# A build-time list scheduler with other durations and due times, the low part of v on GpSimd, row instructions on VectorE alone

## The chip, the core and the metric

The kernel runs on one core of one Trainium2 chip. A core has five engines that work side by side, each through its own queue, in the order in which the program lists its instructions: TensorE (PE; its weight loads are PEld), VectorE (DVE), ScalarE (ACT), GpSimd (POOL) and SyncE (SP), which here only issues DMAs. TensorE writes to PSUM. An engine whose next instruction waits for a semaphore stands still, also when a later instruction of its queue could run. The metric is the device time of one execution in microseconds (us).

## The reference

Three networks follow one another. The first is attention in which a query sees only keys of its own hash bucket (signs of six projections), for 2 batches x 8 heads, 768 positions, head size 64:

```python
q_bits = (np.einsum('bhsd,dk->bhsk', q, proj) > 0).astype(np.int64)
k_bits = (np.einsum('bhsd,dk->bhsk', k, proj) > 0).astype(np.int64)
mask = q_bucket[:, :, :, None] == k_bucket[:, :, None, :]
scores = scale * np.matmul(q, k.transpose(0, 1, 3, 2))
scores = np.where(mask, scores, -1000000000.0)
scores = scores - np.max(scores, axis=-1, keepdims=True)
attn = np.exp(scores)
attn = attn / (np.sum(attn, axis=-1, keepdims=True) + 1e-09)
return np.matmul(attn, v).astype(np.float32)
```

Its output, 2 x 768 x 512, goes through a channel mix (x is blended with the position before, then `k = relu(xk @ w_k)`, `v = k*k @ w_v`, `r = sigmoid(xr @ w_r)`, result `r * v`, inner size 1024), and that through a token mix of rank 32 and a two-matrix MLP (512 to 2048 to 512) with residuals.

## The kernel before

Every operand of a matmul is split into a high and a low part, so that a product is made of three (high x high, high x low, low x high). The weights arrive as 64-bit floats and are put together from their two words by "conversion jobs" (`conv_load`, `conv_scale`, `conv_bits`, `conv_sum`, `conv_h`, `conv_l`), each over SP, ACT, DVE, POOL, ACT and DVE or POOL.

The work has two stages. The first is attention, with the first four conversion jobs and the shift of the first channel mix woven in. It has 16 heads, and each head six tiles of 128 queries, 96 tiles in all. For a head, k and q are loaded (`load_head`), split (`prep_H` makes the high part `hl`, `prep_L` the low one), transposed on TensorE (`prep_T`), copied from PSUM to `yk`, `yq` (`prep_E`), moved by DMA to `xk`, `xq` (`prep_x`), projected (`prep_z`), cut to bits `zt` (`prep_bits`), and the bits are moved by four small DMAs into `xk`, `xq` (`prep_mask`); v is scaled by a power of two (`v_max` to `v_scale`) and split into `V2` (`prep_v`). For a tile n: scores on TensorE into one of three PSUM buffers `ps` (`scores`, L467 and L468), the row maximum (`row_max`, L472, DVE), two instructions on one column (`row_scale`, L476, and `row_bias`, L480), the exponential (`exps`, L486, ACT), and then the split and transposition of the probabilities. Two tiles of six go by TensorE (`flip`, `flip_part1`, `flip_part2`, through a `ps` buffer), four by `part1` (ACT or POOL), `part2` (POOL) and a transposing DMA (`transp`, L501). Last, the probabilities times v (`weighted`, L537, 18 matmuls). After the last head, matmuls of the channel mix begin (`r`), and everything from there on is written out by hand: matmuls on TensorE without a break, with the remaining conversion jobs on the other engines.

The order of the first stage is set by `Plan.order`, a list scheduler that runs while the kernel is built. Each operation is added with its engines and a duration on each, the operations it comes after, a due number (the tile number plus an entry of the table `DUE`), and the buffers that it takes and gives back (`SLOTS`). At each step of a simulated clock the scheduler takes, of the operations that are ready, the one with the lowest due number whose engine and buffers are free; of two engines it takes the one with the shorter duration. The order found is the order of the queues on the chip. DMAs are operations of "sp": the queue is free again 0.1 us after an issue, and the wires are one resource.

## Time and profile before

| What | Value |
|---|---|
| Median of 3 runs | 771.44 us (771.07 to 777.1) |
| The profiled execution: its own time | 771.87 us |
| its span, first to last instruction | 770.1 us |
| mean granted TensorE clock | 0.959 of full speed |
| first and last scores of the first stage | 29.1 and 298.8 us |

The profiled execution's time is 1.8 us above its span and 0.4 us above the median, so sums made on it carry over to the median nearly unchanged. In the rows below an instruction is given as line, engine, operation, and "out<-in" with the names of the tiles.

### The profile page before, as it was taken

To read this page: it belongs to the slowest core of one execution; us is meant where nothing else is said; L and a number is where in the kernel's file an instruction comes from. 1 tells how busy PE (TensorE), PEld (TensorE's weight loads), DVE (VectorE), ACT (ScalarE), POOL (GpSimd) and SP (SyncE) were. 2 spreads that over 40 slices of the span, in tenths; PEclk is the share of its full clock that TensorE was granted. 3 is DMA by queue.
4 is the path that set the end of the run, shared out by engine and by line. 5 is a ranking of instruction groups with operands and counts; after the bars stand their busy time and mean duration, and the time that the engine had idled before them with its cause. 6 is when DMAs were issued, how large, how long until landed. Compare 5 with 4: busy or idle time off the path is not lost.

```text
span 770.1 us, 12423 instructions
## 1 busy us (share of the span) xinstructions
PE 692.0 (90%) x4748; PEld 583.9 (76%) x4748; DVE 479.1 (62%) x778; ACT 372.8 (48%) x607; POOL 367.0 (48%) x365
## 2 busy tenths in 40 slices
PE   3688887887787886999999999999999999999997
PEld 2577777776676775888878888877888888888886
DVE  4776787778989778789977997864643111131112
ACT  3566676665566656586646866643531111111010
POOL 2786797776899778557734754542320000000000
PEclk9598999999989996999999999999999999999999
DMA  8367888886576689233201333232301000010001
GB/s 245 97 134 142 178 190 147 169 154 124 114 144 124 113 185 207 83 123 95 66 28 55 110 113 106 82 110 78 114 28 55 0 1 1 0 55 1 0 1 54
DMA packets 130732, 73.69 MB, mean 96 GB/s; under 512 B 104625, under 2 KB 123953, under 8 KB 130673
## 3 DMA queue, kind: packets, MB, share of 16 engines
q1 hardware_dynamic: 130528, 72.71, 40.0%
q8 instruction: 37, 0.61, 0.3%
q10 hardware_dynamic: 144, 0.20, 0.1%
q14 instruction: 23, 0.18, 0.1%
HBM read 37.10 MB, written 3.15 MB: 52 GB/s over the span
## 4 chain that ended last, share of the span: by engine, by line
PE 60%; DVE 11%; POOL 9%; DMA 9%; issue 5%; ACT 3%; SPq 2%; POOLq 0%; DVEq 0%; ACTq 0%
PE ps L745 9%; PE ps L747 9%; PE ps L746 9%; PE pt L745 7%; PE pt L747 7%; PE pt L746 7%; DMA pT<-p 5%; PE pt L537 3%; POOL p L168 3%; DVE nm L472 2%; DVE w L168 2%; PE ps L467 2%; ACT p L486 2%; PE ps L468 1%; POOL p L352 1%
## 5 line engine op out<-in xcount | busy, mean ns | idle before, releaser
L820 DVE SCALAR_TENSOR_TENSOR hl<-pt,hl 128x512 fp32r<-128x512 f32 x48 | 33.2, 691 | 170.8 <-ACT hl L819 170.8
L819 ACT ACTIVATE hl<-pt 128x512 fp32r<-128x512 f32 x48 | 28.7, 598 | 185.6 <-PE pt L747 185.6
L168 POOL TENSOR_TENSOR cx<-cx,raw 128x512 int32<-128x512 int32 (+2 forms) x55 | 81.6, 1484 | 76.1 <-DVE cx L220 69.5
L747 PE MATMUL ps<-w,hl 128*128 128x512 f32 x288 | 113.6, 395 | 2.7 <-DVE hl L734 2.5
L745 PE MATMUL ps<-w,hl 128*128 128x512 f32 x288 | 114.9, 399 | 1.2 <-ACT y L715 1.1
L746 PE MATMUL ps<-w,hl 128*128 128x512 f32 x288 | 113.1, 393 | 0.0
L168 POOL TENSOR_TENSOR p<-p,p 128x768 f16<-128x768 f32 x64 | 108.4, 1696 | 4.8 <-ACT p L350 2.9
L486 ACT ACTIVATE p<-ps,nm 128x768 f32<-128x768 f32 x96 | 93.6, 989 | 34.1 <-DVE nm L480 14.9
L472 DVE TENSOR_REDUCE nm<-ps 128x1 f32<-128x768 f32 x96 | 90.1, 950 | 29.6 <-PE ps L468 28.3
L467 PE MATMUL ps<-xk,xq 76*128 76x384 f32 x192 | 78.1, 407 | 19.1 <-ACT p L486 12.0
L537 PE MATMUL pt<-v,pT 128*128 128x65 f16 (+1 forms) x1728 | 72.8, 199 | 21.7 <-DMA pT<-p 16.6
L537 PEld LDWEIGHTS <-pT 128*128 128x128 f16 x1728 | 65.5, 102 | 33.6 <-DMA pT<-p 21.8
L745 PE MATMUL pt<-ut,w 128*128 128x512 f32 x192 | 75.5, 393 | 0.0
L747 PE MATMUL pt<-ut,w 128*128 128x512 f32 x192 | 75.0, 391 | 0.0
L746 PE MATMUL pt<-ut,w 128*128 128x512 f32 x192 | 74.9, 390 | 0.0
L468 PE MATMUL ps<-yk,yq 128*128 128x384 f32 x192 | 70.6, 368 | 0.0
L747 PEld LDWEIGHTS ps<-w,hl 128*128 128x128 f32 x288 | 54.0, 188 | 18.3 <-DVE hl L734 6.5
L168 DVE TENSOR_TENSOR w<-cx,w 128x512 fp32r<-128x512 f32 (+2 forms) x53 | 61.8, 1166 | 8.0 <-ACT w L260 5.3
L745 PEld LDWEIGHTS ps<-w,hl 128*128 128x128 f32 x288 | 54.1, 188 | 15.4 <-issue 1.7
L746 PEld LDWEIGHTS ps<-w,hl 128*128 128x128 f32 x288 | 54.1, 188 | 10.2
L467 PEld LDWEIGHTS ps<-xk,xq 76*128 76x128 f32 x192 | 40.7, 212 | 23.4 <-ACT p L486 16.0
L216 DVE SCALAR_TENSOR_TENSOR raw<-raw 128x512 uint32<-128x512 uint32 (+2 forms) x55 | 52.8, 961 | 2.9 <-ACT raw L212 2.9
(166 smaller groups left out, 1417.0 us busy)
## 6 DMA issues: line engine op xcount, KB each, us to landing
raw<-in_moe_w_ch_dram SPq DMA_DIRECT2D x32, 512.0 KB
raw<-in_moe_w_k_dram SPq DMA_DIRECT2D x8, 512.0 KB
raw<-in_moe_w_v_dram SPq DMA_DIRECT2D x8, 512.0 KB
nk<-in_k_dram SPq DMA_DIRECT2D x16, 192.0 KB
nv<-in_v_dram SPq DMA_DIRECT2D x16, 192.0 KB
xk<-yk SPq DMA_DIRECT2D x16, 192.0 KB
xq<-yq SPq DMA_DIRECT2D x16, 192.0 KB
nq<-in_q_dram SPq DMA_DIRECT2D x15, 192.0 KB
```

The costliest lines, as they stand in the source:

```text
L168: eng.tensor_tensor(out=out, in0=a, in1=b, op=op)
L216: nc.vector.scalar_tensor_tensor(out=raw[:, :, 0], in0=raw[:, :, 1], scalar=0x80000000, in1=raw[:, :, 0], op0=ALU.bitwise_and, op1=ALU.bit ...
L467: nc.tensor.matmul(s_ps[:, j, 0:G], d["xq"][:, qc], d["xk"][:, c], start=True, stop=False)
L468: nc.tensor.matmul(s_ps[:, j, 0:G], d["yq"][:, qc], d["yk"][:, c], start=False, stop=True)
L472: nc.vector.tensor_reduce(out=nm[:, 0:1], in_=tl[n]["s"][:, :, 0:G], axis=AX.XY, op=ALU.max, negate=True)
L486: nc.scalar.activation(p, tl[n].pop("s")[:, :, 0:G], AF.Exp, bias=nm[:, 2:3], scale=nm[:, 1:2])
L537: nc.tensor.matmul(o[:, 0:d], pT[:, part, kt, :], V[:, kt, a, 0:d], start=(kt == 0 and (part, a) == (0, 0)), stop=(kt == NT - 1 and part = ...
L745: nc.tensor.matmul(o, sh, mh, start=first, stop=False)
L746: nc.tensor.matmul(o, sh, ml, start=False, stop=False)
L747: nc.tensor.matmul(o, sl, mh, start=False, stop=last)
L819: nc.scalar.activation(hl[:, 0], self.o, AF.Relu)
L820: nc.vector.scalar_tensor_tensor(out=hl[:, 1], in0=self.o, scalar=0.0, in1=f(hl)[:, 0], op0=ALU.max, op1=ALU.subtract)
```

## The change

No arithmetic changes in kind, and the second stage is not touched. Three functions change. `prep_v` made the high part of v on ACT or POOL straight from the loaded v and its scale, and the remainder on DVE with one two-operation instruction that scaled v again; now ACT scales v in place, ACT copies the result to the high part, and POOL subtracts. `row_scale` and `row_bias`, which could go to DVE or POOL, go to DVE alone. In the scheduler, almost all durations and half of `DUE` have other values, an issue on "sp" keeps that queue for 0.5 or 1.4 us, several operations lose one of their engines (the high parts of k and q and the copies to `xT` are ACT's alone after the first head; the shift's first step too), and loads get predecessors: k, q and v of a head, and the early weight loads, wait in the plan for moves of earlier heads.

```diff
-DUE = {"ld": -11, "h": -9, "lo": -6, "tr": -11, "es": -8, "xs": -7, "z": -5, "bits": -8.5, "mask": -5,
+DUE = {"ld": -15, "h": -8.5, "lo": -7, "tr": -11, "es": -8, "xs": -5, "z": -5, "bits": -10.5, "mask": -8,
...
                 if e == "sp":
-                    clock[e] = now + 0.1
-                    wire = max(wire, now + 1.3) + cost
-                    op.end = wire + 0.8
+                    clock[e] = now + (1.4 if cost > 2.2 else 0.5)
+                    wire = max(wire, now + 1.2) + cost
+                    op.end = wire + 0.6
...
-    def prep_v(i, part, e):
-        v, sc, h = hd[i]["nv"], v_scale_of(i), V2[i % 2][:, :, 0, 0:D]
-        if part:
-            nc.vector.scalar_tensor_tensor(
-                out=V2[i % 2][:, :, 1, 0:D], in0=v, scalar=sc, in1=h, op0=ALU.mult, op1=ALU.subtract
-            )
-            hd[i].pop("nv")
-        elif e == "act":
-            nc.scalar.activation(h, v, AF.Identity, scale=sc)
+    def prep_v(i, part):
+        v, h = hd[i]["nv"], V2[i % 2][:, :, 0, 0:D]
+        if part == 0:
+            nc.scalar.activation(v, v, AF.Identity, scale=v_scale_of(i))
+        elif part == 1:
+            nc.scalar.activation(h, v, AF.Copy)
         else:
-            nc.gpsimd.tensor_scalar(h, v, sc, None, ALU.mult)
+            minus("pool", V2[i % 2][:, :, 1, 0:D], hd[i].pop("nv"), h)
...
-        due = i * NT
+        due = i * NT if i else -50
         y_done, xs, masks, toks = [], [], [], {}
+        gate = ready_of[max(i - 2, 0)][1] if i else []
...
-            ld = add({"sp": 0.8}, lambda e, i=i, s=s: i and load_head(i, s), due=due + DUE["ld"] if i else -99, take=[n_s])
-            h = add({"act": 0.52, "dve": 0.4}, lambda e, i=i, s=s: prep_H(i, s, e), [ld], due + DUE["h"], take=[hl_s])
+            ld = add({"sp": 0.8}, lambda e, i=i, s=s: i and load_head(i, s), gate, due + DUE["ld"] if i else -99, take=[n_s])
+            h = add({"act": 0.53, "dve": 0.4} if i == 0 else {"act": 0.53}, lambda e, i=i, s=s: prep_H(i, s, e), [ld], due + DUE["h"], take=[hl_s])
...
-                v1 = add({"act": 0.52, "pool": 0.55}, lambda e, i=ii: prep_v(i, 0, e), [v_sc, v_ld[ii]], d + DUE["v1"], take=[v_s2])
-                v2_of[ii] = add({"dve": 0.6}, lambda e, i=ii: prep_v(i, 1, e), [v1], d + DUE["v2"], free=[nv_s2])
+                v0 = add({"act": 0.52}, lambda e, i=ii: prep_v(i, 0), [v_sc, v_ld[ii]], d + DUE["v1"] - 0.5)
+                v1 = add({"act": 0.52}, lambda e, i=ii: prep_v(i, 1), [v0], d + DUE["v1"], take=[v_s2])
+                v2_of[ii] = add({"pool": 1.0}, lambda e, i=ii: prep_v(i, 2), [v1], d + DUE["v2"], free=[nv_s2])
...
-            sl = add({"dve": 0.165, "pool": 0.25}, lambda e, n=n: row_scale(n, e), [mx], n + DUE["sl"])
-            bi = add({"dve": 0.225, "pool": 0.3}, lambda e, n=n: row_bias(n, e), [sl], n + DUE["bi"])
+            sl = add({"dve": 0.17}, lambda e, n=n: row_scale(n), [mx], n + DUE["sl"])
+            bi = add({"dve": 0.23}, lambda e, n=n: row_bias(n), [sl], n + DUE["bi"])
...
-        last = ld = add({"sp": 2.1}, lambda e, j=j: conv_load(j), [last_s[-10] if j >= KD else None], due - 10, take=[raw_s])
+        last = ld = add({"sp": 2.1}, lambda e, j=j: conv_load(j), [last_s[-10] if j >= KD else ready_of[j][0][0]], due - 10, take=[raw_s])
```

Counted over the queues: DVE loses 19 high parts of k and q, 9 copies to `xT`, all 16 remainders of v and 12 shift multiplications, and gains 86 row instructions; POOL loses those 86 and 8 scalings of v and gains the 16 subtractions; ACT gains the 19, the 9, the shift's and, for v, has 32 instructions where it had 8. In TensorE's queue the scores that stand ahead of a tile's `weighted` are, over tiles 6 to 89, 5.65 more than its own number before and 6.60 now.

On SyncE, at the start of the program, before (tiles carry their buffer numbers; `raw` is a weight, `nk`, `nq` and `nv` are loads of heads; the last two rows are the mask moves of head 0):

```order
L199 DMA raw_168<-in_moe_w_r_dram 128x1024
L292 DMA nk_179<-in_k_dram 128x384
L292 DMA nq_193<-in_q_dram 128x384
L387 DMA xk_202<-yk_185 64x768
L387 DMA xq_205<-yq_200 64x768
L292 DMA nk_234<-in_k_dram 128x384
L292 DMA nq_242<-in_q_dram 128x384
L199 DMA raw_257<-in_moe_w_r_dram 128x1024
L387 DMA xk_268<-yk_238 64x768
L387 DMA xq_277<-yq_249 64x768
L407 DMA xk_202<-zt_220 12x384 x2
L407 DMA xq_205<-zt_220 12x384 x2
```

The same place now (its rows three to six are the moves of head 0):

```order
L574 DMA mu_k_142<-in_moe_mu_k_dram 128x4x1
L574 DMA mu_r_145<-in_moe_mu_r_dram 128x4x1
L387 DMA xk_175<-yk_163 64x768
L387 DMA xq_178<-yq_173 64x768
L407 DMA xk_175<-zt_189 12x384 x2
L407 DMA xq_178<-zt_189 12x384 x2
L292 DMA nv_195<-in_v_dram 128x384
L292 DMA nv_197<-in_v_dram 128x384
L292 DMA nk_199<-in_k_dram 128x384
L292 DMA nq_201<-in_q_dram 128x384
L199 DMA raw_208<-in_moe_w_r_dram 128x1024
L292 DMA nv_215<-in_v_dram 128x384
```

The moves of head 0 now stand ahead of every load but those of head 0 and of three small tensors; before, 16 loads of heads and weights stood ahead of the mask moves, six of them in this block.

On DVE, some 33 tiles into the first stage, before (`nm` holds a tile's maximum, scale and bias):

```order
L472 TENSOR_REDUCE nm_1781<-ps_1764 128x1
L476 TENSOR_SCALAR nm_1781<-nm_1781 128x1
L472 TENSOR_REDUCE nm_1808<-ps_1783 128x1
L544 TENSOR_SCALAR rl_1821<-pt_1564,vsc_1460 128x6
L449 SCALAR_TENSOR_TENSOR v2_0_132<-nv_325,vsc_1460,v2_0_132 128x6x64
L548 RECIPROCAL rl_1821<-rl_1821 128x6
L556 TENSOR_TENSOR xn_1831<-pt_1564,rl_1821 128x6x64
L168 TENSOR_TENSOR pT_1833<-ps_1810,pT_1833 128x768
L472 TENSOR_REDUCE nm_1867<-ps_1835 128x1
L472 TENSOR_REDUCE nm_1880<-ps_1869 128x1
L417 TENSOR_REDUCE vmax_388<-nv_1829 128x1
L352 CAST hl_k_1938<-nk_1392 128x6x64
```

The same place now (L469, L473 and L477 are maximum, scale and bias):

```order
L469 TENSOR_REDUCE nm_1660<-ps_1640 128x1
L473 TENSOR_SCALAR nm_1660<-nm_1660 128x1
L469 TENSOR_REDUCE nm_1689<-ps_1662 128x1
L477 TENSOR_SCALAR nm_1660<-nm_1660 128x1
L473 TENSOR_SCALAR nm_1689<-nm_1689 128x1
L477 TENSOR_SCALAR nm_1689<-nm_1689 128x1
L469 TENSOR_REDUCE nm_1748<-ps_1720 128x1
L473 TENSOR_SCALAR nm_1748<-nm_1748 128x1
L477 TENSOR_SCALAR nm_1748<-nm_1748 128x1
L400 TENSOR_SCALAR zt_1777<-pt_1753,thr_118 108x384
L469 TENSOR_REDUCE nm_1788<-ps_1770 128x1
L473 TENSOR_SCALAR nm_1788<-nm_1788 128x1
```

Now each maximum is followed by both row instructions within a few places; before, four maxima have one row instruction here, the others were POOL's or stand behind a later maximum.

On ACT, around the exponentials of tiles 24 to 27, before:

```order
L486 ACTIVATE p_1400<-ps_1360,nm_1371 128x768
L350 ACTIVATE p12_1448<-p_1400 128x768
L486 ACTIVATE p_1458<-ps_1374,nm_1394 128x768
L454 ACTIVATE v2_0_132<-nv_154,vsc_1460 128x6x64
L486 ACTIVATE p_1477<-ps_1384,nm_1446 128x768
L486 ACTIVATE p_1511<-ps_1453,nm_1474 128x768
L350 ACTIVATE p12_1536<-p_1511 128x768
L520 ACTIVATE pT_1545<-ps_1529 128x768
```

The same place now (L449 scales a loaded v in place, L451 makes its high part):

```order
L483 ACTIVATE p_1398<-ps_1276,nm_1321 128x768
L350 ACTIVATE hl_q_1425<-nq_1248 128x6x64
L449 ACTIVATE nv_230<-nv_230,vsc_1432 128x384
L449 ACTIVATE nv_397<-nv_397,vsc_1432 128x384
L451 ACTIVATE v2_0_132<-nv_230 128x6x64
L449 ACTIVATE nv_734<-nv_734,vsc_1432 128x384
L449 ACTIVATE nv_1033<-nv_1033,vsc_1432 128x384
L483 ACTIVATE p_1472<-ps_1393,nm_1434 128x768
L483 ACTIVATE p_1520<-ps_1427,nm_1450 128x768
L451 ACTIVATE v2_1_134<-nv_397 128x6x64
```

Four instructions for v, and one for q, now stand in a row between two exponentials, and a fifth behind the pair that follows.

## Rows read from the trace of the kernel before

**Rows 1.** The page: the chain that ended last, by engine.
```profile
PE 60%; DVE 11%; POOL 9%; DMA 9%; issue 5%; ACT 3%; SPq 2%; POOLq 0%; DVEq 0%; ACTq 0%
```

**Rows 2.** Stretches: length, busy time by engine (instructions), clock, DMA share.
```profile
0.00:29.00 29.00, 12.81 (x45) 9.42 (x46) 16.61 (x53) 12.44 (x24) 12.36 (x18) 0.81 0.73 208
29.00:304.00 275.00, 221.23 (x2546) 196.97 (x2545) 217.53 (x399) 178.01 (x255) 215.53 (x239) 0.91 0.74 148
304.00:330.00 26.00, 24.91 (x192) 20.74 (x192) 18.39 (x26) 15.83 (x30) 16.07 (x14) 0.99 0.39 106
330.00:770.00 440.00, 433.02 (x1968) 356.73 (x1968) 226.59 (x302) 166.53 (x301) 123.08 (x96) 1.00 0.17 55
```

**Rows 3.** The chain, 29 to 304 us, by line.
```profile
by line: DMA pT<-p 14.3%; issue 7.9%; POOL p L168 7.5%; PE pt L537 7.5%; DVE nm L472 6.8%; PE ps L467 5.0%; ACT p L486 4.4%; PE ps L468 4.0%; POOL p L352 3.8%; SPq L407 3.7%; PE pt L376 2.8%; DMA nv<-in_v_dram 2.5%; DMA raw<-in_moe_w_v_dram
```

**Rows 4.** Waits, 29 to 304 us: us in total, times, longest.
```profile
PE pt L537 <- DMA pT<-p: 16.6, 13, 4.2
...
ACT p L486 <- DVE nm L480: 14.9, 14, 2.9
...
ACT p L486 <- POOL nm L480: 14.2, 14, 2.7
...
PE ps L467 <- ACT p L486: 12.0, 11, 3.5
```

**Rows 5.** SyncE's queue, its longest wait, same columns.
```profile
SPq L501 <- POOL nm L480: 24.9, 11, 4.5
```

**Rows 6.** Groups, 0 to 420 us: busy us, mean ns; idle before, releasers.
```profile
L449 DVE SCALAR_TENSOR_TENSOR v<-nv,vsc,v 128x384 f16<-128x384 f32 x16 | 17.9, 1120 | 3.3 <-POOL v L456 2.9 <-ACT v L454 0.4
...
L168 POOL TENSOR_TENSOR hl_k<-nk,hl_k 128x384 fp32r<-128x384 f32 x15 | 16.4, 1090 | 15.5 <-DMA raw<-in_moe_w_r_dram 12.4 <-DVE hl_k L352 2.8 <-ACT hl_k L350 0.3
...
L480 POOL TENSOR_SCALAR nm<-nm 128x1 f32<-128x1 f32 x45 | 13.9, 311 | 4.0 <-DVE nm L476 1.7
...
L476 POOL TENSOR_SCALAR nm<-nm 128x1 f32<-128x1 f32 x41 | 11.1, 271 | 14.9 <-DVE nm L472 12.4 <-DVE nm L476 1.3 <-DVE rl L548 0.7
L456 POOL TENSOR_SCALAR v<-nv,vsc 128x384 f16<-128x384 f32 x8 | 10.8, 1353 | 2.3 <-DVE vsc L440 1.4 <-PE pt L537 0.9
...
L480 DVE TENSOR_SCALAR nm<-nm 128x1 f32<-128x1 f32 x51 | 10.4, 209 | 1.6 <-POOL nm L476 0.2
...
L476 DVE TENSOR_SCALAR nm<-nm 128x1 f32<-128x1 f32 x55 | 8.1, 148 | 0.8
...
L352 DVE CAST hl_q<-nq 128x384 fp32r<-128x384 f32 x9 | 6.4, 712 | 3.1 <-PE pt L376 3.1
...
L352 DVE CAST hl_k<-nk 128x384 fp32r<-128x384 f32 x11 | 5.6, 512 | 2.3 <-POOL p L352 1.5 <-PE pt L376 0.7
...
L352 DVE COPY xT<-pt 128x384 f32<-128x384 f32 x9 | 5.0, 552 | 2.1 <-PE pt L566 1.8
L454 ACT ACTIVATE v<-nv,vsc 128x384 f16<-128x384 f32 x8 | 4.9, 610 | 5.3 <-PE pt L537 4.9 <-DVE vsc L440 0.4
...
L350 ACT ACTIVATE hl_q<-nq 128x384 fp32r<-128x384 f32 x7 | 3.6, 517 | 1.3 <-DMA nq<-in_q_dram 1.3
```

**Rows 7.** Timeline of the start: start, length, instruction.
```profile
7.92 0.56 DVE L168 TENSOR_TENSOR hl_k<-nk,hl_k 128x384 fp32r<-128x384 f32 x1
...
14.29 0.68 DVE L400 TENSOR_SCALAR zt<-ps,thr 108x384 fp32r<-108x384 f32 x1 [3.96 <-PE ps L396]
...
21.42 1.70 SPq L407 DMA_DIRECT2D xk<-zt  x2
...
23.16 1.47 SPq L407 DMA_DIRECT2D xq<-zt  x2
...
28.57 0.88 PE L376 MATMUL pt<-ident,hl_k 128*128 128x128 f32 x3 [1.68 <-DVE zt L400]
```

**Rows 8.** Score matmuls: ns min/median/max, first and last start.
```profile
L467 PE MATMUL ps<-xk,xq x192: 335/414/690, 29.1 to 298.8; 76*128 76x384 f32 x192
```

**Rows 9.** Transposing DMAs on SyncE, same columns.
```profile
L501 SPq DMA_TRANSPOSE pT<-p x64: 1304/1556/5523, 38.0 to 309.8; - x64
```

More of the change, by code (lines that the diff above doesn't have):

```diff
@@ L875, in lsh_attention_moe_kernel @@
         zt_s, z_s = Slot("zt"), Slot("t" if i else "s")
-        z = add({"pe": 1.48}, lambda e, i=i: prep_z(i), y_done, due + DUE["z"], take=[z_s], lag=0.25)
-        bits = [add({"dve": 0.57}, lambda e, i=i: prep_bits(i), [z], due + DUE["bits"], take=[zt_s], free=[z_s])]
+        z = add({"pe": 1.5}, lambda e, i=i: prep_z(i), y_done, due + DUE["z"], take=[z_s], lag=0.25)
+        bits = [add({"dve": 0.69}, lambda e, i=i: prep_bits(i), [z], due + DUE["bits"], take=[zt_s], free=[z_s])]
         for s in ("k", "q"):
@@ L921, in lsh_attention_moe_kernel @@
                 c_s = Slot("p12")
-                p1 = add({"act": 0.87, "pool": 0.85}, lambda e, n=n: part1(n, e), [ex], n + DUE["p1"], take=[c_s])
-                p2 = add({"pool": 1.7}, lambda e, n=n: part2(n), [p1], n + DUE["p2"], free=[p_s])
+                p1 = add({"act": 0.86, "pool": 0.86}, lambda e, n=n: part1(n, e), [ex], n + DUE["p1"], take=[c_s])
+                p2 = add({"pool": 1.72}, lambda e, n=n: part2(n), [p1], n + DUE["p2"], free=[p_s])
                 got = add({"sp": 2.3}, lambda e, n=n: transp(n), [p2], n + DUE["T"], take=[pT_s], free=[c_s])
@@ L943, in lsh_attention_moe_kernel @@
         raw_s, cx_s = Slot("raw"), Slot("cx")
-        last = ld = add({"sp": 2.1}, lambda e, j=j: conv_load(j), [last_s[-10] if j >= KD else None], due - 10, take=[raw_s])
+        last = ld = add({"sp": 2.1}, lambda e, j=j: conv_load(j), [last_s[-10] if j >= KD else ready_of[j][0][0]], due - 10, take=[raw_s])
         if j < JOBS_EARLY + 3:
-            last = add({"act": 1.36}, lambda e, j=j: conv_scale(j), [ld], due, take=[cx_s])
+            last = add({"act": 1.35}, lambda e, j=j: conv_scale(j), [ld], due, take=[cx_s])
         if j < JOBS_EARLY + 2:
-            last = add({"dve": 1.6}, lambda e, j=j: conv_bits(j), [last], due + 1)
+            last = add({"dve": 1.75}, lambda e, j=j: conv_bits(j), [last], due + 1)
         if j < JOBS_EARLY + 1:
@@ L952, in lsh_attention_moe_kernel @@
             h = add({"act": 0.65}, lambda e, j=j: conv_h(j), [last], due + 3)
-            last = add({"dve": 1.2, "pool": 1.3}, lambda e, j=j: conv_l(j, e), [h], due + 4, free=[cx_s])
+            last = add({"dve": 1.1, "pool": 1.4}, lambda e, j=j: conv_l(j, e), [h], due + 4, free=[cx_s])
     tick_n[0] = JOBS_EARLY + 3
```

34 lines of the change are left out of this document (17 added, 17 removed).

## The prediction

> **What bounds the kernel now.** I read the chain of the whole execution first, then busy time by stretch, then the same chain and the waits inside the first stage. The chain by engine gives TensorE 60% and splits the rest over VectorE, GpSimd, DMA, issue and ScalarE [rows 1]; it says that two kernels lie behind one another. The stretches show them. From 330 us on TensorE is busy for 433.0 of 440 us at full clock, and the change does not touch that code, so those 440 us stay, as do the 26 us in which the mix's first matmuls fill TensorE beside the last tiles (24.9 of 26 busy) [rows 2]. The prediction is about the first 304 us.
>
> Between 29 and 304 us no engine is full: TensorE 221.2, VectorE 217.5, GpSimd 215.5 and ScalarE 178.0 of 275 us, the DMA engines 0.74 [rows 2]. TensorE stands still for 275 - 221.2 = 53.8 us. The chain in that stretch has no dominant line either: landing transposes 14.3%, GpSimd's subtractions 7.5%, the row maximum 6.8%, the exponential 4.4% [rows 3]. The scores run from 29.1 to 298.8 us, 96 tiles, so 269.7 / 96 = 2.81 us for a tile [rows 8]. A stage like this is bound by queues that stand behind the wrong instruction, and by latency from tile to tile. The reader should take from the waits which pairs these are: TensorE's product with v waits for a transposing DMA 13 times, 16.6 us in all and at most 4.2; its scores wait for an exponential, which frees their PSUM buffer, 12.0 us; and the exponential in turn waits for a row instruction, 14.9 us on VectorE and 14.2 on GpSimd [rows 4]. GpSimd's row instructions also end the longest waits of SyncE's transposes, 24.9 us [rows 5].
>
> **The start.** Head 0's bits are ready at 14.29 + 0.68 = 14.97 us, but their four moves leave between 21.42 and 24.63 us, because loads stand ahead of them; then TensorE's queue waits for head 1's bits and the first score starts at 29.1 [rows 7, 8]. In the new queue nothing stands between. Four issues take 1.70 + 1.47 = 3.17 us, so they are out at 18.1, and with some 2 us to land (an estimate: from the last issue's end at 24.63 to the matmul at 28.57 is at most 3.9) the first score starts near 20, 9 us earlier. But the loads of head 1 now leave after these moves and not before, so its split starts later than it did, and head 0's six tiles at 2.81 us are over at 37. From there the lead counts only as far as head 1 is ready. Bounds are 0 and -9; I take -4, below the middle, since head 1's whole preparation now lies beside head 0's tiles.
>
> **Engine loads.** VectorE loses the remainders of v (17.9 us), 10 x 0.512 + 9 x 0.712 = 11.5 for the high parts and 5.0 for copies to `xT`, and gains 41 x 0.148 + 45 x 0.209 = 15.5 of row instructions: -18.9 [rows 6]. GpSimd loses 13.9 + 11.1 + 10.8 = 35.8 and gains 16 subtractions, which I price with those of `hl_k` of the same shape, 16 x 1.09 = 17.4: -18.4 [rows 6]. ScalarE gains 19 x 0.517 for high parts, 9 x 0.517 for copies, and 16 x (0.610 + 0.517) - 4.9 = 13.1 for v: +27.6 [rows 6]. The first step of the shift adds a little to the last and takes it from the first. Over the 275 us VectorE goes from 79% to 72%, GpSimd from 78% to 72%, ScalarE from 65% to 75%. No total falls much; the loads get even. Three conversions that ran in the first 29 us come in on top. I price the added ScalarE work at +3: bounds are 0, if it fits into ScalarE's 97 idle us, and +14, if half of it comes between a maximum and its exponential. The value is nearer to zero because of that idle time.
>
> The row on the moved remainder is double-edged. On VectorE it took 1.12 us, while a subtraction of that shape ahead of the stage, when GpSimd had nothing to do, took 0.56 [rows 6, 7]. The Trainium skill (GPSIMD Engine Reference, 4.1 Engine selection) says to keep two-input elementwise work on VectorE, GpSimd being about twice as slow, which speaks against this move. The trace agrees for the lone pair, 0.56 against 1.09, and not for the instruction as it ran.
>
> **Row instructions.** An exponential that waits for GpSimd's row instruction waits for one that is queued behind that engine's subtractions and casts. On VectorE both now follow their maximum within a few places, each shorter by 0.1 us (0.209 for 0.311, 0.148 for 0.271) [rows 6]. The 14.2 us of waiting on GpSimd can go; new waiting on VectorE comes, where a second maximum stands ahead. Of the exponential's waits only a part reaches TensorE: the scores' 12.0 us [rows 4]. Bounds are 0 and -12; I take -5, the share of GpSimd in the two waits (14.2 of 29.1) of those 12.0, rounded down.
>
> **Slack for the transposes.** In the new TensorE queue a product with v stands 0.95 tiles further behind its scores, 6.60 against 5.65 tiles, which is 0.95 x 2.81 = 2.7 us more time for subtraction, issue and landing. The 13 waits average 1.28 us and the longest is 4.2 [rows 4], so most are shorter than the added slack. What is late next is the buffers: the transposed tiles have six, and a queue that runs 6.6 tiles behind fills them, so a transpose may wait for a buffer in place of a product for a transpose. Bounds are 0 and -16.6; I take -10. This rests on the scheduler's longer issue for transposes (1.4 us for 0.1), and the trace supports that number: 64 transposes take 1.56 us at the median to issue [rows 9]. It also shows where the new numbers are still short: two mask moves are counted as one issue of 0.5 us and take 1.47 to 1.70 [rows 7].
>
> **The sum.** -4 + 3 - 5 - 10 = -16 us on the profiled execution's 771.87, hence 755.9; the median of the runs is 0.4 us lower, so I say 756. With every bound on its good side it would be 771.9 - 9 - 12 - 16.6 = 734, with every bound on its bad side 771.9 + 14 = 786.
>
> **Rivals.** First, DMA sets the pace. The transposes take 64 x 1.56 = 100 us of issue, the mask moves 16 x 3.17 = 51, and landing transposes are the largest single line of the chain [rows 3, 7, 9]; none of it is changed. Then only the start is left: 768. Against it, SyncE waits for others for long stretches and the DMA engines have a quarter of their time free [rows 2, 5].
>
> Second, and on the other side, ScalarE stops the exponentials. High parts of k and q are ScalarE's alone, and the loads that they need now leave one head later in SyncE's queue; ScalarE runs in order, so a cast that waits for its load holds the exponentials behind it, and with them the PSUM buffers of the scores. At 14 heads and 2 us each (an estimate, half of the 3.9 us above from a DMA's issue to the matmul behind it) that is +28, against the -16: 784. It decides from the point at which a load is issued less than its landing time ahead of the cast; TensorE's 12.0 us of waiting on exponentials shows that such a delay goes straight through [rows 4]. Against it, the plan puts a head's casts some two tiles, or 5.6 us, behind its loads.
>
> Third, the order pays more than its parts: half of TensorE's 53.8 idle us goes, -27, and the start -4: 741. For it, no engine is above 80%; against it, none falls below 72%, and every queue still runs in order.
>
> Fourth, VectorE's relief is half as large, as the lone 0.56 us would have it: then 16 x 0.56 = 9.0 and not 17.9 us leave VectorE, 9 us come back, and if all of it is on the path the time is 765. The page named above gives that rule.
>
> Fifth, the scheduler's new numbers are no nearer to the chip than the old, as with the mask moves, and the stage keeps its 2.81 us a tile: 771.
>
> **How the numbers follow.** Forecast, 750 to 762: 0.45. DMA's pace, 768: 0.18. ScalarE holds the exponentials, 784: 0.10. Half the idle time, 741: 0.19. The halved relief, 765: 0.05. No difference, 771: 0.03. About 1% (7.7 us) is what a measurement of this kernel can tell from no change, so faster begins below 763.7: the forecast and the third rival, 0.65 rounded; within 1% 0.25; slower 0.10. The range reaches from 739 to 770: it leaves out the ScalarE rival, the last, and the far part of the third.
>
> **What would show it.** The first score near 20 us and head 1's first near 37; the last score near 283; scores (283 - 20) / 96 = 2.74 us apart in between. TensorE's waits for transposes below 10 us; no exponential waiting for GpSimd; GpSimd's busy time in the stage some 18 us lower and ScalarE's some 28 higher. The stretch behind the last head as long as before, 466 us from the first mix matmul to the end. The prediction is wrong if ScalarE's casts show waits for `nk` or `nq` with exponentials behind them, or if the tiles keep their 2.81 us while all of the above waits are gone, which would mean that a wait has only changed its name.

## The result, and the profile after

The changed kernel takes 740.75 us (median of four runs, 740.09 to 746.55), the kernel before beside it 771.66 us. The ratio is 0.9601, with a 95% interval of 0.9536 to 0.9666: 31 us less, where 756 us were forecast, in a range of 739 to 770. The profiled execution took 740.09 us with a span of 738.3, against 771.87 and 770.1.

The page of the changed kernel, the chain by engine [rows 1]:

```profile
PE 67%; DVE 12%; DMA 8%; ACT 5%; issue 3%; POOL 3%; SPq 2%; DVEq 0%; ACTq 0%; POOLq 0%
```

Its stretches, cut at the first score, the first mix matmul and 26 us later (columns as in [rows 2]):

```profile
0.00:18.00 18.00, 4.57 (x21) 3.91 (x21) 5.28 (x32) 3.37 (x6) 0.95 (x10) 0.92 0.22 48
18.00:270.00 252.00, 215.56 (x2551) 191.89 (x2552) 197.26 (x444) 204.71 (x324) 202.04 (x168) 0.95 0.84 176
270.00:296.00 26.00, 26.00 (x205) 21.79 (x205) 22.37 (x30) 18.13 (x34) 19.52 (x15) 0.92 0.49 141
296.00:738.00 442.00, 433.90 (x1975) 357.64 (x1973) 229.04 (x305) 168.79 (x305) 126.30 (x98) 1.00 0.18 56
```

GpSimd has nearly left the chain (9% to 3%), and the second stage is what it was, 433.90 us of TensorE for 433.02 [rows 2]. Between the first score and the first mix matmul GpSimd was busy 202.04 us for 215.53, VectorE 197.26 for 217.53 and ScalarE 204.71 for 178.01, 13.5 and 20.3 less and 26.7 more, where 18, 18.9 and 28 had been forecast.

The score matmuls and the transposing DMAs of the changed kernel (columns as in [rows 8, 9]):

```profile
L464 PE MATMUL ps<-xk,xq x192: 336/344/689, 18.0 to 263.7; 76*128 76x384 f32 x192
...
L498 SPq DMA_TRANSPOSE pT<-p x64: 1280/1480/5388, 27.5 to 277.7; - x64
```

The scores split the gain. The first one comes 11.1 us earlier (18.0 for 29.1). From there to the last one it is 245.7 us for 269.7, 24.0 less, or 2.56 us a tile for 2.81. From the last one to the end of the span it is 738.3 - 263.7 = 474.6 us for 471.3, 3.3 more. Together that is -31.8, the difference of the spans. But the lead of the first score isn't kept. The first line here is the changed kernel's first score; the other two are the first score of head 1, the seventh tile, in the changed kernel and in the kernel before:

```profile
17.99 0.66 PE L464 MATMUL ps<-xk,xq 76*128 76x384 f32 x1 [4.63 <-DMA xq<-zt]
...
37.81 0.41 PE L464 MATMUL ps<-xk,xq 76*128 76x384 f32 x1 [0.23 <-DMA xq<-zt]
```
```profile
41.40 0.34 PE L467 MATMUL ps<-xk,xq 76*128 76x384 f32 x1
```

So 3.6 us are won up to head 1, 31.5 from there to the last score, and 3.3 are given back behind it. Most of it lies in the second half of the tiles, in which the shift is woven in. The windows from the 49th tile to the 73rd and on to the last, of the kernel before and then of the changed one:

```profile
158.10:233.10 75.00, 59.95 (x662) 52.64 (x662) 62.72 (x111) 45.25 (x72) 60.45 (x68) 0.89 0.68 134
233.10:298.00 64.90, 51.30 (x645) 45.31 (x645) 54.21 (x97) 42.42 (x59) 52.23 (x57) 0.95 0.78 156
```
```profile
148.10:210.00 61.90, 54.45 (x666) 48.43 (x666) 52.31 (x117) 51.63 (x89) 54.50 (x47) 0.97 0.85 169
210.00:263.30 53.30, 48.96 (x624) 43.74 (x624) 40.93 (x100) 45.02 (x69) 41.39 (x34) 0.97 0.71 160
```

The two windows from the first to the last tile, of the kernel before and then of the changed one, show what the tiles lost:

```profile
29.10:298.00 268.90, 216.97 (x2517) 193.28 (x2515) 212.88 (x390) 173.57 (x249) 209.76 (x233) 0.92 0.74 147
```
```profile
18.00:263.30 245.30, 212.49 (x2523) 189.37 (x2523) 191.94 (x436) 199.15 (x316) 196.37 (x164) 0.95 0.83 175
```

TensorE stood still 51.9 us before and 32.8 now, 19.1 less; the other 4.5 us are matmuls that ran faster, at a granted clock of 0.95 for 0.92. Over the whole execution, in which every kernel here has the same 4,748 matmuls, TensorE stood still 19.9 us less (58.3 for 78.1) and its matmuls took 11.9 us less (680.0 for 692.0), at a mean granted clock of 0.977 for 0.959. The kernel before and then the changed one:

```profile
0.00:770.10 770.10, 691.97 (x4748) 583.86 (x4748) 479.10 (x778) 372.82 (x607) 367.03 (x365) 0.96 0.40 96
```
```profile
0.00:738.30 738.30, 680.03 (x4748) 575.23 (x4748) 453.95 (x808) 394.99 (x668) 348.81 (x290) 0.98 0.41 100
```

The waits from the first to the last tile, of the kernel before as far as [rows 4] doesn't show them for this window, and then of the changed kernel:

```profile
ACT p L486 <- POOL nm L480: 12.6, 13, 2.7
...
PE ps L512 <- ACT p L486: 5.6, 9, 1.1
...
PE ps L467 <- DMA xk<-zt: 1.9, 1, 1.9
...
PE pt L376 <- ACT yk L350: 1.8, 2, 1.0
...
PE ps L467 <- DMA xq<-zt: 1.5, 2, 1.1
```

```profile
PE pt L534 <- DMA pT<-p: 10.7, 11, 2.0
...
PE ps L464 <- DMA xq<-zt: 10.1, 8, 4.6
...
ACT p L483 <- DVE nm L477: 5.2, 8, 1.3
...
PE ps L464 <- ACT p L483: 1.5, 4, 0.6
```

Scores that wait for an exponential, 12.0 us before, are nearly gone (1.5), and the exponential's own wait for a row instruction has fallen from 14.9 + 12.6 to 5.2, on VectorE alone. The waits for transposes have fallen from 16.6 only to 10.7. Of the 10.1 us in which scores wait for a head's mask moves, 4.6 are the first score's own wait, which ends where the window begins; the other 5.5 stand against 1.9 + 1.5 before.

### The profile page after: what moved, and what is told of

Read it like the earlier page. It is cut to its first block, busy times and chain, and to the rows that moved or that the text cites. A ratio compares the mean times of both kernels' runs of the same rounds, so it can differ in the third digit from the quotient of the medians.

```text
span 738.3 us, 12386 instructions
## 1 busy us (share of the span) xinstructions
PE 680.0 (92%) x4748; PEld 575.2 (78%) x4748; DVE 453.9 (61%) x808; ACT 395.0 (54%) x668; POOL 348.8 (47%) x290
## 4 chain that ended last, share of the span: by engine, by line
PE 67%; DVE 12%; DMA 8%; ACT 5%; issue 3%; POOL 3%; SPq 2%; DVEq 0%; ACTq 0%; POOLq 0%
PE ps L742 9%; PE ps L744 9%; PE ps L743 9%; PE pt L742 8%; PE pt L744 8%; PE pt L743 8%; DMA pT<-p 4%; PE pt L534 3%; PE ps L464 3%; PE ps L465 3%; PE pt L396 2%; DMA xq<-zt 2%; DVE w L168 2%; SPq L407 2%; DVE raw L216 2%
## 5 line engine op out<-in xcount | busy, mean ns | idle before, releaser
L469 DVE TENSOR_REDUCE nm<-ps 128x1 f32<-128x768 f32 x96 | 90.4, 951 | 24.7 <-PE ps L465 21.6
L464 PE MATMUL ps<-xk,xq 76*128 76x384 f32 x192 | 75.2, 392 | 12.5 <-DMA xq<-zt 10.1
L534 PE MATMUL pt<-v,pT 128*128 128x65 f16 (+1 forms) x1728 | 69.4, 196 | 13.7 <-DMA pT<-p 12.6
L534 PEld LDWEIGHTS <-pT 128*128 128x128 f16 x1728 | 62.5, 99 | 24.0 <-DMA pT<-p 17.4
L744 PEld LDWEIGHTS ps<-w,hl 128*128 128x128 f32 x288 | 54.1, 188 | 18.2 <-DVE hl L731 6.3
L465 PE MATMUL ps<-yk,yq 128*128 128x384 f32 x192 | 68.0, 354 | 0.0
L216 DVE SCALAR_TENSOR_TENSOR raw<-raw 128x512 uint32<-128x512 uint32 (+2 forms) x55 | 54.5, 991 | 0.3 <-ACT raw L212 0.2
L464 PEld LDWEIGHTS ps<-xk,xq 76*128 76x128 f32 x192 | 38.6, 201 | 18.2 <-issue 6.1
```

Source lines behind the costliest of these rows:

```text
L216: nc.vector.scalar_tensor_tensor(out=raw[:, :, 0], in0=raw[:, :, 1], scalar=0x80000000, in1=raw[:, :, 0], op0=ALU.bitwise_and, op1=ALU.bit ...
L464: nc.tensor.matmul(s_ps[:, j, 0:G], d["xq"][:, qc], d["xk"][:, c], start=True, stop=False)
L465: nc.tensor.matmul(s_ps[:, j, 0:G], d["yq"][:, qc], d["yk"][:, c], start=False, stop=True)
L469: nc.vector.tensor_reduce(out=nm[:, 0:1], in_=tl[n]["s"][:, :, 0:G], axis=AX.XY, op=ALU.max, negate=True)
L534: nc.tensor.matmul(o[:, 0:d], pT[:, part, kt, :], V[:, kt, a, 0:d], start=(kt == 0 and (part, a) == (0, 0)), stop=(kt == NT - 1 and part = ...
L744: nc.tensor.matmul(o, sl, mh, start=False, stop=last)
```

## The experiments

Two kinds of edit were made. The first leaves the list that the scheduler made as it is and changes one thing in it; the second changes numbers of the plan and lets the scheduler make another list. Theories are named by letters where they come up. The table holds every run: "slack" is the mean number of tiles by which TensorE's queue is ahead in scores when a product with v comes; the stretch, idle time and busy time of TensorE are those from the first to the last tile; the last columns are TensorE's waits for a transpose and for an exponential that frees a score buffer. All but slack and time are those of the profiled execution; for jit_after (747.64 us) and mask_cost (747.47 us) that one is the fastest of four, 4 to 5 us below the median.

| Kernel | slack | stretch | idle | busy | transpose | exponential | time, ratio to before (95%) |
|---|---|---|---|---|---|---|---|
| before | 5.65 | 268.9 | 51.9 | 217.0 | 16.6 | 12.0 | 771.66 |
| changed | 6.60 | 245.3 | 32.8 | 212.5 | 10.7 | 1.5 | 740.75, 0.9601 (0.9536 to 0.9666) |
| rows_pool | 6.60 | 259.9 | 37.1 | 222.8 | 8.3 | 8.7 | 751.93, 0.9731 (0.9696 to 0.9766) |
| v_old | 6.60 | 249.6 | 36.1 | 213.6 | 10.0 | 2.9 | 743.54, 0.9629 (0.9591 to 0.9668) |
| av_early | 5.88 | 277.1 | 51.5 | 225.6 | 21.6 | 3.0 | 768.76, 0.9953 (0.9929 to 0.9976) |
| av_late | 6.56 | 277.1 | 56.3 | 220.8 | 1.9 | 16.4 | 783.11, 1.0148 (1.0106 to 1.0190) |
| rows_only | 5.65 | 272.3 | 57.4 | 214.9 | 18.8 | 14.9 | 775.46, 1.0045 (1.0020 to 1.0069) |
| rows_late | 6.56 | 279.2 | 57.6 | 221.7 | 1.5 | 19.3 | 784.15, 1.0166 (1.0122 to 1.0211) |
| start_exec | 5.65 | 294.2 | 64.1 | 230.1 | 17.4 | 14.9 | 785.52, 1.0179 (1.0144 to 1.0213) |
| due_old | 5.63 | | | | | | 769.55, 0.9942 (0.9912 to 0.9973) |
| jit_after | 6.35 | 252.1 | 39.0 | 213.1 | 16.7 | 1.4 | 752.33, 0.9736 (0.9700 to 0.9773) |
| jit_before | 5.77 | 263.2 | 55.5 | 207.7 | 17.3 | 12.8 | 767.43, 0.9949 (0.9922 to 0.9976) |
| sp_old | 6.64 | 256.7 | 43.0 | 213.7 | 14.8 | 11.0 | 755.14, 0.9791 (0.9767 to 0.9814) |
| mask_cost | 6.61 | 253.7 | 36.0 | 217.7 | 8.9 | 8.5 | 751.29, 0.9740 (0.9688 to 0.9792) |

Two of the nine executions of due_old, the profiled one among them, took 1688 us, the other seven 765.8 to 770.7; nothing is read from its trace, and why it happens isn't known.

**The row instructions, given back (rows_pool), in the order of the changed kernel.**

```diff
-        nc.vector.tensor_scalar(nm[:, 1:2], nm[:, 0:1], MASK_C * 0.5, scale, ALU.is_lt, ALU.mult)
+        (nc.gpsimd if n % 2 else nc.vector).tensor_scalar(nm[:, 1:2], nm[:, 0:1], MASK_C * 0.5, scale, ALU.is_lt, ALU.mult)
...
-        nc.vector.tensor_scalar(nm[:, 2:3], nm[:, 0:1], P_SHIFT / scale, nm[:, 1:2], ALU.add, ALU.mult)
+        (nc.gpsimd if n % 2 else nc.vector).tensor_scalar(nm[:, 2:3], nm[:, 0:1], P_SHIFT / scale, nm[:, 1:2], ALU.add, ALU.mult)
```

> The changed kernel with every queue's order kept but for this: of every second tile the two row instructions (scale and bias) run on GpSimd, as about half of them did before, 96 instructions in all. Theory A, slack (the transposes' wait was the largest term): the order of TensorE's queue and the slack are those of the changed kernel, so most of the gain stays: 743 to 746 us. Theory B, the row instructions (an exponential that waits for GpSimd holds a PSUM buffer of the scores): exponentials wait some 14 us for GpSimd again, TensorE's scores wait again for exponentials by 10 us and more: 750 to 756 us.

It took 751.93 us, as theory B said; theory A is missed. Its window and waits from the first to the last tile:

```profile
18.40:278.30 259.90, 222.79 (x2522) 199.12 (x2523) 183.97 (x342) 200.38 (x317) 219.22 (x259) 0.90 0.82 168
```
```profile
ACT p L483 <- POOL nm L477: 17.5, 23, 2.4
...
PE ps L464 <- ACT p L483: 8.7, 10, 1.9
...
PE pt L534 <- DMA pT<-p: 8.3, 8, 2.2
```

The exponential waits for GpSimd again, 17.5 us, and the scores for the exponential, 8.7. But only 4.3 of the 14.6 us by which the stretch is longer are idle time of TensorE (37.1 for 32.8). The other 10.3 are the same matmuls at a granted clock of 0.90 for 0.95.

**The split of v, as before (v_old), in the order of the changed kernel.**

```diff
-            nc.scalar.activation(v, v, AF.Identity, scale=v_scale_of(i))
+            pass
...
-            nc.scalar.activation(h, v, AF.Copy)
+            nc.scalar.activation(h, v, AF.Identity, scale=v_scale_of(i))
...
-            minus("pool", V2[i % 2][:, :, 1, 0:D], hd[i].pop("nv"), h)
+            nc.vector.scalar_tensor_tensor(
+                out=V2[i % 2][:, :, 1, 0:D], in0=hd[i].pop("nv"), scalar=v_scale_of(i), in1=h, op0=ALU.mult, op1=ALU.subtract
+            )
```

> The changed kernel with the split of v made as before at the places of the new order: ScalarE makes the high part from the loaded v and its scale in one instruction, VectorE the remainder, GpSimd's 16 subtractions are gone. Theories A (slack) and B (row instructions): within 3 us of the changed kernel, 738 to 744 us. Theory C, the engines' loads (VectorE's relief is what pays): VectorE gets 16 instructions of about 1.1 us back, some 18 us, of which a quarter to a half shows: 745 to 749 us.

It took 743.54 us, and the two intervals overlap: what the new split is worth by itself can't be told from nothing. Theory C's range is missed, and so is its premise: over the whole execution VectorE was busy 465.0 us for 454.0 in the changed kernel, so it got 11 us back and not 18. As 2.8 is a quarter of 11, this refutes its size and not its rule. VectorE's 16 remainders took 777 ns on average (1120 before [rows 6]), with a median of 609:

```profile
L453 DVE SCALAR_TENSOR_TENSOR v<-nv,vsc,v x16: 597/609/1439, 40.7 to 258.9; 128x384 f16<-128x384 f32 x16
```

The eight of them during which GpSimd stood idle took 597 to 609 ns; the other eight 606 to 1439. GpSimd's subtraction in the changed kernel took 957 ns.

**The products with v, moved alone (av_early, av_late).** A pass over the finished list moves a product across one score of TensorE's queue, unless something that it needs, or that needs it, stands between. Here is that of av_early; av_late is its mirror image on the kernel before, with a condition more for the buffers of the transposed tiles and of v.

```diff
+            avs[-1].av, sc.sc, (p1 if t in PE_TILES else got).pT = n, n, n
...
-    for op, e in plan.order():
+    seq = plan.order()
+    pos = 0
+    while pos < len(seq):
+        op = seq[pos][0]
+        if hasattr(op, "av"):
+            j = pos - 1
+            while not hasattr(seq[j][0], "sc"):
+                j -= 1
+            if op.av % NT and not any(x in op.after or hasattr(x, "av") for x, _ in seq[j:pos]):
+                seq.insert(j, seq.pop(pos))
+        pos += 1
+    for op, e in seq:
```

> The changed kernel, in which the products with v are moved one score forward in TensorE's queue where nothing that they need forbids it: the slack falls from 6.60 to 5.88 tiles, no other queue is touched. Theory A (slack): TensorE's waits for transposes grow from some 30 us with the weight loads' to over 40, and the time to 747 to 751 us. Theory B (row instructions): the scores come a place later and the waits stay nearly where they are, 740 to 744 us.

It took 768.76 us: 28 of the 31 us are gone, with nothing changed but the place of some products in one queue. The wait for transposes is twice as long, 21.6 us for 10.7, as theory A said, but the loss is far above its 6 to 10 us; theory B is missed too. TensorE idles 51.5 us for 32.8, 18.7 more, and its matmuls take 13.1 us more at a clock of 0.91.

> The kernel before, in which the products with v are moved one score back in TensorE's queue where the buffers allow it: the slack rises from 5.65 to 6.56 tiles, as in the changed kernel, and nothing else changes. Theory A (slack): TensorE's wait for transposes falls by 10 us: 761 to 764 us. Theory B (row instructions): the scores wait for exponentials as before, or longer since they now come earlier: 768 to 773 us.

The opposite step on the kernel before took 783.11 us, 11 more. Its waits from the first to the last tile:

```profile
ACT p L486 <- DVE nm L480: 21.6, 17, 4.1
...
PE ps L467 <- ACT p L486: 16.4, 15, 3.6
...
PE ps L512 <- ACT p L486: 9.8, 12, 2.6
ACT p L486 <- POOL nm L480: 9.5, 10, 3.2
...
PE pt L376 <- ACT yk L350: 7.8, 4, 4.0
...
PE pt L376 <- ACT yq L350: 5.9, 6, 2.1
...
PE pt L537 <- DMA pT<-p: 1.9, 2, 1.1
```

The wait for transposes is gone, 1.9 us for 16.6, just as the prediction had it. Not a microsecond of it was won: scores wait 16.4 us for exponentials for 12.0, the transposes that go by TensorE 9.8 for 5.6 (L512), those of k and q 13.7 for ScalarE's copies of the ones before them, for 1.8 (L376), and TensorE idles 56.3 us for 51.9. Theory A is out as an account of the gain, and the time lies above theory B's range as well.

**The row instructions alone, and with later products (rows_only, rows_late), in the order of the kernel before.** rows_late adds the pass of av_late to this:

```diff
-        (nc.vector if e == "dve" else nc.gpsimd).tensor_scalar(nm[:, 1:2], nm[:, 0:1], MASK_C * 0.5, scale, ALU.is_lt, ALU.mult)
+        nc.vector.tensor_scalar(nm[:, 1:2], nm[:, 0:1], MASK_C * 0.5, scale, ALU.is_lt, ALU.mult)
...
-        (nc.vector if e == "dve" else nc.gpsimd).tensor_scalar(nm[:, 2:3], nm[:, 0:1], P_SHIFT / scale, nm[:, 1:2], ALU.add, ALU.mult)
+        nc.vector.tensor_scalar(nm[:, 2:3], nm[:, 0:1], P_SHIFT / scale, nm[:, 1:2], ALU.add, ALU.mult)
```

> The kernel before with every queue's order kept but for this: the 86 row instructions that ran on GpSimd run on VectorE, at their place in the same list. It is the mirror image of the run in which the changed kernel gave half of them back to GpSimd and lost 11 us. Theory P, the parts add up: the same 11 us come here: 759 to 763 us. Theory Q, the order decides what a part is worth (TensorE's queue of before has its products with v too early, and a relief elsewhere only turns into a wait for transposes): within 5 us of before, 767 to 773 us.

It took 775.46 us, 3 more than the kernel before beside it (772.48) and 2 above the range that theory Q gave: within its 5 us, and theory P is out. The step that is worth 11 us in one order is worth nothing in the other. Its waits show why:

```profile
ACT p L486 <- DVE nm L480: 35.6, 28, 4.3
...
PE pt L537 <- DMA pT<-p: 18.8, 14, 5.0
PE ps L467 <- ACT p L486: 14.9, 14, 3.5
```

The exponential's 12.6 us on GpSimd are gone and those on VectorE rose from 14.9 to 35.6. The wait has changed its name and grown. VectorE is busy 217.7 of 272.3 us here, and its queue was made for fewer row instructions, so that one now stands behind whatever the scheduler put there for another reason; that this is the cause is read from the list and not tested.

> The kernel before with both: the row instructions on VectorE, and the products with v one score later in TensorE's queue (slack 6.56). The later products alone had taken away the waits for transposes and cost 11 us all the same, because scores and exponentials then waited for each other. Theory Q1, the two need each other: later products pay only where the exponentials no longer wait for GpSimd, so this one is clearly below the run with the row instructions alone: 750 to 760 us. Theory Q2, later products hurt whatever the row instructions do, since the scores come earlier than the buffers: the 11 us are added to that run: 770 to 783 us.

784.15 us: theory Q2, a microsecond above its range; later products cost 9 us more here as well. Theory Q1, that the two steps need each other and nothing else, is out.

**The start alone (start_exec), before the order of the kernel before.**

```diff
+            sc.sc, ex.sc = n, 3 + n
...
-    for op, e in plan.order():
+    seq = plan.order()
+    early, grow = set(), [op for op, e in seq if getattr(op, "sc", 9) < 4]
+    while grow:
+        op = grow.pop()
+        if op is not None and op not in early:
+            early.add(op)
+            grow += op.after
+    seq = [x for x in seq if x[0] in early] + [x for x in seq if x[0] not in early]
+    for op, e in seq:
```

> The kernel before with one change of order at the start: all that the first four scores of head 0 and the first exponential need stands ahead of everything else in every queue, so that the mask moves of head 0 leave before the loads of later heads, as in the changed kernel. From the fifth tile on the order is that of before. The first score should come near 18 us and not 29. If the start is worth the 4 us of the prediction: 766 to 769 us. If it is all given back by head 1's later loads: 770 to 773 us. If all 11 us stay: 759 to 762 us.

The first score came at 17.7 us, 11.4 earlier, and the kernel took 785.52 us, 13 more; none of the three expectations held. The timeline of ScalarE, and below it one line of TensorE (start, length, instruction):

```profile
21.09 0.99 ACT L486 ACTIVATE p<-ps,nm 128x768 f32<-128x768 f32 x1 [9.06 <-POOL nm L480]
23.61 0.66 ACT L211 ACTIVATE cx<-raw 128x512 f32<-128x512 f32 x1 [1.53 <-DMA raw<-in_moe_w_r_dram]
...
44.69 0.63 ACT L231 ACTIVATE w<-cx 128x512 fp32r<-128x512 f32 x1 [2.45 <-POOL cx L168]
45.23 0.97 ACT L486 ACTIVATE p<-ps,nm 128x768 f32<-128x768 f32 x1
```
```profile
46.26 0.69 PE L467 MATMUL ps<-xk,xq 76*128 76x384 f32 x1 [5.31 <-ACT p L486]
```

The second exponential stands in ScalarE's queue where the old list put it, behind the preparation of two heads and several conversion jobs, whose loads now leave after the mask moves. So it ran at 45.23 us, and the fifth tile's scores, which need its buffer, at 46.26, where the kernel before has them at 36.3. Head 1's first score is 11.4 us behind the kernel before (52.8 for 41.4) and the last one 13.9 (311.9 for 298.0): what was lost in the first tiles is still missing at the last. A start that is pulled ahead in one place pays only if what the first tiles need later is pulled ahead with it.

**The plan's numbers (due_old, sp_old, jit_after, jit_before, mask_cost).** due_old gives the changed kernel the due numbers of the kernel before, sp_old the old model of SyncE's queue.

```diff
-DUE = {"ld": -15, "h": -8.5, "lo": -7, "tr": -11, "es": -8, "xs": -5, "z": -5, "bits": -10.5, "mask": -8,
-       "vm": -14, "v1": -3, "v2": -2, "sc": -1.5, "mx": -0.5, "sl": -1, "bi": -4, "ex": 0, "fl": 2.5,
-       "f1": 0.5, "f2": -3.5, "p1": 2.5, "p2": 1, "T": 0, "av": 6, "nr": -0.5, "xp": 7.5, "xe": 3, "job": 25,
-       "mix": 6}
+DUE = {"ld": -11, "h": -9, "lo": -6, "tr": -11, "es": -8, "xs": -7, "z": -5, "bits": -8.5, "mask": -5,
+       "vm": -14, "v1": -3, "v2": -2, "sc": -1.5, "mx": -0.5, "sl": -1, "bi": -1, "ex": -1, "fl": 2.5,
+       "f1": 0.5, "f2": -0.5, "p1": 2.5, "p2": 3, "T": 0, "av": 3, "nr": 0, "xp": 6, "xe": 3, "job": 16,
+       "mix": 12}
```

> The changed kernel with the table of due numbers of before, all durations and the rest as in the changed kernel; the scheduler makes another order out of them, with a slack of 5.63 tiles, nearly that of before. Theory R, the order of TensorE's queue carries most of the gain (as the 28 us lost with earlier products say): 757 to 770 us, with over 20 us of waits for transposes. Theory S, the row instructions and the queues' new durations carry it, and those 28 us came because only one queue was moved and the others not with it: 740 to 748 us.

769.55 us, theory R: with the old due numbers all the rest of the change together (the new durations, the row instructions on VectorE, the new split of v, the gates on the loads) is worth half a per cent. Whether the new due numbers alone, with all the rest as before, would do it was not run. Since there is no trace of an ordinary execution, which queue's order does it stays open; that the slack fell to 5.63 fits TensorE's, but does not show it. The step of sp_old:

```diff
-                    clock[e] = now + (1.4 if cost > 2.2 else 0.5)
-                    wire = max(wire, now + 1.2) + cost
-                    op.end = wire + 0.6
+                    clock[e] = now + 0.1
+                    wire = max(wire, now + 1.3) + cost
+                    op.end = wire + 0.8
```

> The changed kernel with the old model of SyncE's queue (an issue keeps it 0.1 us, not 0.5 or 1.4), all other numbers as in the changed kernel; slack 6.64. Theory M, with the issue times as what makes the plan true: 755 to 768 us, with TensorE's waits for transposes back above 16 us. Theory D: somewhere among the neighbours, no more than with the step in the exponential: within 5 us of that run.

755.14 us. That alone would be theory M, but its sign is missing: the wait for transposes is 14.8 us, below 16, the slack as large as in the changed kernel. And a step that says nothing about SyncE gives nearly the same time, jit_after:

```diff
-            ex = add({"act": 1.02}, lambda e, n=n: exps(n), [bi], n + DUE["ex"], take=[p_s], free=[s_s, nm_s])
+            ex = add({"act": 1.03}, lambda e, n=n: exps(n), [bi], n + DUE["ex"], take=[p_s], free=[s_s, nm_s])
```

> The changed kernel, in which the plan counts an exponential as 1.03 us and not as 1.02; nothing else. The scheduler makes a somewhat different order of it (slack 6.35). Theory M, the model: durations read from the trace make the plan true, and any order made with them is good: 738 to 747 us. Theory D, the draw: the order of the changed kernel is one good one among many that numbers like these give, and its neighbours lie between it and the kernel before: 750 to 770 us.

752.33 us, theory D. Ten nanoseconds on one number of the plan cost 12 us. The profiled execution shows 7.5 of them (747.64 for 740.09), and what grew most was the wait for transposes:

```profile
PE pt L534 <- DMA pT<-p: 16.7, 14, 2.3
...
ACT pT L517 <- PE ps L509: 5.9, 11, 1.3
ACT p L483 <- DVE nm L477: 5.8, 7, 2.7
```

> The kernel before with the same step, 1.03 for 1.02 us in the plan. Theory M: the old model gives orders near the old time: 768 to 778 us. Theory D: the order of before is a draw as well, and its neighbours scatter by 10 us or more, to either side: below 765 or above 780 us.

The same step on the kernel before gave 767.43 us, 4 to 5 less and just below what theory M allowed; a scatter of 10 us, as theory D had it, was not seen there. The last step is mask_cost:

```diff
-                    clock[e] = now + (1.4 if cost > 2.2 else 0.5)
+                    clock[e] = now + (1.4 if cost > 2.2 or cost < 0.5 else 0.5)
```

> The changed kernel, in which the plan counts the two issues of a mask move as 1.4 us and not 0.5, which is what they take (1.5 to 1.7 us); slack 6.61. In the changed kernel scores wait 10 us for mask moves. Theory M: a truer plan is a better one: 733 to 740 us. Theory D: a neighbour like the others, 745 to 770 us.

751.29 us, and theory M is out as far as it says that a truer number gives a better order. The waits of mask_cost from the first to the last tile:

```profile
ACT p L483 <- DVE nm L477: 18.4, 14, 3.2
...
PE pt L534 <- DMA pT<-p: 8.9, 9, 1.6
PE ps L464 <- ACT p L483: 8.5, 12, 1.6
...
PE ps L464 <- DMA xq<-zt: 5.4, 2, 4.6
```

Without the first score's wait of 4.6 us, which both have, the wait for mask moves is nearly gone, 0.8 us for 5.5, and the exponentials wait 18.4 us for 5.2 in its place. No kernel tried here beats the changed one.

The three neighbours of the changed kernel (jit_after, sp_old, mask_cost) lie at 751 to 755 us. Read that way, some 17 to 20 of the 31 us belong to what these four kernels share, the other new numbers of the plan and the moved instructions, and the other 11 to 14 to this one order among its neighbours. Three are few, two of them change more than a last digit, and the kernel before has a neighbour 4 to 5 us below it as well, so the split is rough.

## Why the prediction was right in direction and too small

The direction and the range held, for only a part of the reasons. The largest error is one of form: "-4 + 3 - 5 - 10 = -16" adds up four parts as if each had a price of its own. rows_pool against rows_only, and av_early against av_late, show that they have none: giving half of the row instructions back cost 11 us in the new order, and taking them all over gained nothing in the old one; moving products forward cost 28 us in the new order, and moving them back cost 11 in the old. What was changed is the order as a whole, and the third rival, "the order pays more than its parts", 741 us at a chance of 0.19, is what came. That its figure was met is partly luck. Its price was half of the 53.8 idle us, -27, and the start, -4; what went over the whole execution were 19.9 idle us, four more than the 16 of the sum, and 11.9 us by which the same matmuls ran faster, for which neither had a term. The range held by 1.8 us.

**The start, -4.** The first score came at 18.0 us (forecast near 20). Of the 11.1 us, 3.6 were left at head 1's first score, which came at 37.8 (forecast near 37): this term was right in size and in mechanism, as the lead counted only as far as head 1 was ready. start_exec is no test of it: it had the same first score, but held up the second exponential.

**Engine loads, +3.** v_old gives the share of v: 2.8 us in the new split's favour, not to be told from nothing. No run takes back the casts and copies that went to ScalarE, so the term as a whole isn't measured. The fourth rival (VectorE's relief halved, 765 us) had the better premise: the new split relieves VectorE by 11 us in v_old's comparison, and not by 17.9. Its price is out, since all of that cost no more than 2.8. The busy times between the first score and the first mix matmul came within 1.5 us of the forecast for VectorE and ScalarE and 5 beside it for GpSimd, but this is in part luck, because work that stood ahead of the first score before now lies behind it (VectorE's busy time there fell from 16.6 us to 5.3). Over the whole execution VectorE lost 25.2 us (forecast 18.9), GpSimd 18.2 (18.4), and ScalarE gained 22.2 (27.6). The subtraction on GpSimd took 0.957 us where 1.09 was taken from `hl_k` [rows 6]. The Trainium skill (GPSIMD Engine Reference, 4.1 Engine selection) says to keep two-input elementwise work on VectorE, with GpSimd about twice as slow. The trace agrees in direction: in the same order VectorE's remainder, which also scales v, took 777 ns on average and 597 to 609 beside an idle GpSimd, against 957. The 1120 ns that the prediction set against it are those of the order before.

**Row instructions, -5.** The mechanism was right and the size was off in the changed order. Exponentials wait for no row instruction on GpSimd any more, the scores' 12.0 us of waiting fell to 1.5, and half of the row instructions back on GpSimd cost 11 us. The step that failed is "of the exponential's waits only a part reaches TensorE: the scores' 12.0 us". The 11 us lie within that bound but are made up otherwise: 10.3 of the 14.6 us by which rows_pool's stretch is longer are matmuls at a lower clock, and only 4.3 are idle time. The price holds in that order alone, as rows_only shows.

**Slack for the transposes, -10.** This was the largest term, and it was wrong twice. First, "this rests on the scheduler's longer issue for transposes": with the old issue times (sp_old) the slack is 6.64, with the old due numbers (due_old) 5.63. It rests on the due number of the product, 6 for 3, or on others of that table. Second, the wait fell by 5.9 us and not by 10; "below 10 us" was not reached. And where the slack alone was raised (av_late), the wait went away and the time rose. "What is late next" was named as the transposed tiles' buffers; in av_late it was ScalarE, with the exponentials that free the score buffers and the copies of transposed k and q.

**The clock** has no term in the sum, which takes TensorE's busy time as fixed, although [rows 2] shows 0.81 and 0.91 ahead of the mix and 1.00 in it. It is the larger part of what the forecast lacked: 11.9 of the 31.8 us are the same matmuls in less time in the profiled executions, 4.5 of them from the first to the last tile, where rows_pool and av_early took 10.3 and 13.1 us more than the changed kernel.

**The other rivals.** DMA's pace (768) is out: the transposes still take 1.48 us of issue at the median and the stretch is 24 us shorter. ScalarE held up hardly an exponential by a late load: of the 10.3 us in which `hl_k` waits for `nk` in the changed kernel, 9.9 are one wait at the start, and the first exponential behind it began at 23.43 us, half a microsecond after its bias was there. The tiles did not keep their 2.81 us, so the fifth rival (771) is out too. From the first mix matmul to the end it is 738.3 - 269.7 = 468.6 us, for the 466 that were said:

```profile
269.73 0.78 PE L742 MATMUL ps<-w,xh 128*128 128x512 f32 x1
```

## What to carry to other kernels

In a stage in which no engine is full and every queue runs in order, don't add up the waits that a change removes: undo one part in the new order and do it alone in the old one; if the two don't agree, the part has no price of its own. Before a list scheduler's gain is put down to a truer model, move one of its numbers by a per cent and look at the neighbours; here some 11 to 14 of 31 us were this one order. A wait for one releaser that goes to nothing proves little as long as the idle time of the engine that bounds the stage stands where it stood.
